# A gated GLU on one core: unit 1's weights from ACT's queue to the end of SP's transposing loads, and t2 ahead of s1 and s2

## Chip, cores and metric

The kernel runs on one core of a Trainium2 chip. The metric is the device time in microseconds of one execution; three executions of the kernel before took 551.66, 552.02 and 553.04 us, the median being 552.02.

A core has five engines that run their own instruction streams and wait for each other by semaphores: PE (TensorE: matmuls out of SBUF into PSUM banks), DVE (VectorE), ACT (ScalarE), POOL (GpSimd) and SP (SyncE, which here only issues DMAs). DMAs are issued from the queue of SP or of ACT, in the order of that queue, and the transfers run on 16 DMA engines.

## The reference

```python
B, S, Dm, Df = 1, 2048, 1024, 3584

def reference(x, w_gate, w_up, w_down):
    g = jnp.einsum("bsd,df->bsf", x, w_gate)
    u = jnp.einsum("bsd,df->bsf", x, w_up)
    h = _gelu(g) * u                      # gelu, tanh form
    return jnp.einsum("bsf,fd->bsd", h, w_down)
```

All arrays are bf16.

## The kernel before

The 2048 rows of x are worked in two passes (`ip`) of 1024 rows, each pass in two halves of 512 rows (`c` = 0 and 1; the "second rows" of the change are half 1 of pass 0). x is kept transposed: `xT[c]` has Dm on the partitions, in 8 blocks of 128 (`ko`). Df is worked in 14 units of 256 columns. For each unit a tile `w` holds 256 columns of w_gate and of w_up (two DMAs of 512 KB, `load_w`); the pool of these tiles has three buffers.

A unit's product is made by Strassen's scheme in Winograd's form: seven block products in place of eight, out of sums of blocks. Sums of x's blocks are `t1` to `t4` (four instructions each) and a cast `tb`; sums of the weights' blocks are `s1` to `s4` (two each, one for gate and one for up) and a cast `sa`. Sums are `TENSOR_TENSOR` instructions with both inputs in SBUF: DVE makes them through the helper of line 90, POOL through that of line 93. The casts are ACT's (line 102). t2 needs t1, s2 needs s1, t4 needs t2, s4 needs s2. After the products DVE adds PSUM banks to snapshots (`sum<-bank,p`, `bank<-bank,p`), ACT applies the gelu, and DVE multiplies gate by up into `hT`.

Unit 0 of pass 0 is different: it is made by plain products (`plain`), first for half 0 and then for half 1, so that PE has work while the sums of x and of unit 1's weights are made. The start goes like this:

- SP's queue: four loads of x's first 512 rows (line 436), which PE transposes (line 443); six loads of unit 0's weights (line 453); eight transposing DMAs for half 1 of x, one for each `ko` (line 447); then, in the units that follow, the weights two units ahead and two loads of w_down's rows per unit (`raw`, line 256).
- ACT's queue: the two loads of unit 1's weights (line 503, issued by `load_w` at line 121), placed after ACT's copy of a transposed block. Then gelu of unit 0's first half, the casts `tb` and `sa`, gelu of the second half, two snapshots, and the two loads of unit 2's weights (line 543, called from `aside(-1)` at the head of unit 1).
- PE: `plain` for half 0 (16 matmuls of 256 columns, 24 of 512), `plain` for half 1 (32 of 512 columns, four banks for each pair of `ko`), then unit 1: its first product (8, out of `w` and half 0 of x), another 8, then s2 by t2, s1 by t1, s3 by t3, s4 by tb, the first product of unit 2, and sa by t4 (8 each).
- DVE: t1, hT of half 0, s1, s2, t2, t3, s3, hT of half 1, two adds, s4, t4, and then the unit's sums and products.

The sums `s` of unit 2 and all later units are made by POOL (`make_s(ahead, pool)`, line 530), which in pass 0 also makes sums `m` of w_down's blocks (`keep`, lines 268 to 270), one `j` per unit and three in the last one (the last two into tiles named `w`). SP stores these to a scratch tensor `td` in HBM (lines 277 and 279). The down projection of the pass (`down`) starts with plain products of hT and raw rows of w_down that SP loads (`fetch12`, line 328) from an agenda by step; three such loads stand in SP's queue ahead of the last stores of `td`, the others behind them.

The order on SP, DVE, POOL and PE is the order in which the program is written, and so is ACT's within the start (`manual_schedule`). Small tiles (`t`, `s`, `g`, `raw` and so on) share one pool of 52 slots.

Of the kernel before, what the change touches and what calls it, by code (L numbers as in the profile page):

```python
# [10 lines left out]
def kernel(  # L11
# [23 lines left out]
    nc = tc.nc  # L35
# [40 lines left out]
    def new_x():  # L76
        return [xpool.tile([P, NKB, N], bf16, name=f"xT{c}") for c in range(2)]
# [17 lines left out]
    def new(eng, a, b, op, name, shape=None, dtype=None):  # L95
        t = slot(shape or [P, N], dtype or f32r, name)
        eng(t, a, b, op)
        return t

    def cast(src, name, shape=None):  # L100
        t = slot(shape or [P, N], f32r, name)
        nc.scalar.copy(out=t, in_=src)  # L102
        return t
# [10 lines left out]

    def load_w(u, queue=nc.sync, pinned=False):
        f0 = u * 2 * P
        w = wpool.tile([P, 2, NKB, 2 * P], bf16, name="w")
        for i, src in enumerate((w_gate, w_up)):  # L120
            got = queue.dma_start(
                out=w[:, i],
                in_=src[:, f0 : f0 + 2 * P].rearrange("(ko ki) f -> ki ko f", ki=P),
            )
            if queue is not nc.sync and not pinned:
                tc.keep_in_program_order(got)
        return w

# [7 lines left out]
    def sums_t(xT):  # L136
        K = range(KH)
        lo, hi = [[xT[c][:, k] for k in K] for c in range(2)], [
            [xT[c][:, KH + k] for k in K] for c in range(2)
        ]  # L140
        return Sums(
            how={
                "t1": lambda q: [new(dve, lo[1][k], lo[0][k], SUB, "t1") for k in K],
                "t2": lambda q: [new(dve, hi[1][k], q["t1"][k], SUB, "t2") for k in K],
                "t3": lambda q: [new(dve, hi[1][k], lo[1][k], SUB, "t3") for k in K],
                "t4": lambda q: [new(dve, hi[0][k], q["t2"][k], SUB, "t4") for k in K],
                "tb": lambda q: [cast(hi[1][k], "tb") for k in K],
            }
        )

    def sums_s(w, eng):
        GU = range(2)
        sh = [P, KH, P]
        a11, a21 = [[w[:, i, :KH, h : h + P] for i in GU] for h in (0, P)]
        a12, a22 = [[w[:, i, KH:, h : h + P] for i in GU] for h in (0, P)]
        return Sums(
            how={
                "s1": lambda q: [new(eng, a21[i], a22[i], ADD, "s1", sh) for i in GU],
                "s2": lambda q: [new(eng, q["s1"][i], a11[i], SUB, "s2", sh) for i in GU],
                "s3": lambda q: [new(eng, a11[i], a21[i], SUB, "s3", sh) for i in GU],  # L160
                "s4": lambda q: [new(eng, a12[i], q["s2"][i], SUB, "s4", sh) for i in GU],
                "sa": lambda q: [cast(a22[i], "sa", sh) for i in GU],
            }
        )
# [11 lines left out]
    def gelu(src):  # L176
        g = slot([P, N], f32, "g")
        nc.scalar.activation(g, src, ACT.Gelu_apprx_tanh)  # L178
        return g

    def times(fb, c, g, u):
        dve(hT[:, fb // NJ, fb % NJ, c, :], g, u, MUL)
# [257 lines left out]
    def turn(xT, xn, c, i, copy):  # L440
        tp = bank[4 + i].bitcast(bf16).rearrange("p (k r) -> p k r", k=NKB)
        for ko in range(NKB):
            nc.tensor.transpose(tp[:, ko, :], xn[i][:, ko * P : (ko + 1) * P], ident)
        copy(out=xT[c][:, :, i * P : (i + 1) * P], in_=tp)
# [17 lines left out]
    xT = new_x()  # L462
# [7 lines left out]
    def plain(ps, c, kos, parts=1):  # L470
        n = N // parts
        for k in range(kos.start, kos.stop, 2):
            for part in range(parts):
                cols = slice(part * n, (part + 1) * n)
                for p, (j, i) in zip(ps, [(j, i) for j in range(2) for i in range(2)]):
                    for ko in (k, k + 1):
                        matmul(
                            p[:, cols],
                            wf[:, i, ko, j * P : (j + 1) * P],
                            xT[c][:, ko, cols],  # L480
                            ko == 0 and part == 0,
                            ko == NKB - 1,
                        )

    def finish(ps, c):
        for j in range(2):
            times(j, c, gelu(ps[2 * j]), ps[2 * j + 1])

    on_dve, on_act = nc.vector.tensor_copy, nc.scalar.copy
    t = sums_t(xT)  # L490
    with tc.manual_schedule(engines={ENG.Activation}):
        def keep_warm(n, cols):
            for _ in range(n):
                nc.tensor.matmul(
                    bank[3][:, :cols], lhsT=warm[:, :P], rhs=warm[:, :cols], start=True, stop=True
                )

        keep_warm(NWARM, N)
        for i in range(NS):
            turn(xT, xn0, 0, i, on_act if i == 1 else on_dve)  # L500
            if i < NS - 1:
                keep_warm(3, 2 * P)
        w = load_w(1, nc.scalar, pinned=True)
        s = sums_s(w, dve)
        plain(bank[0:4], 0, range(0, 2), parts=2)
        plain(bank[0:4], 0, range(2, NKB))
        t.make("t1")
        finish(bank[0:4], 0)
        s.make("s1", "s2")
        t.make("t2", "t3", "tb")  # L510
        s.make("s3", "sa")
        plain(bank[4:8], 1, range(NKB))
        finish(bank[4:8], 1)
# [8 lines left out]
    for ip in range(NPASS):  # L522
        for u in range(1 if ip == 0 else 0, NU):
            js = making(u) if ip == 0 else []

            def prepare():
                nonlocal ahead
                nxt["w"], nxt["s"] = ahead, None
                if u + 1 < NU:
                    nxt["s"] = make_s(ahead, pool)  # L530
                if u + 2 < NU:
                    ahead = load_w(u + 2)
                if ip == 0:
                    fetch_wd(making(u + 1))
                    for j in making(u - 1):
                        store_made(j)
                for j, home in zip(js, ("m",) if len(js) == 1 else ("slots", "w", "w")):
                    keep(j, home)

            def aside(part):  # L540
                nonlocal ahead
                if ahead is None:
                    ahead = load_w(2, nc.scalar)
                if part == 0 and "s4" not in s:
                    s.make("s4")
                    t.make("t4")
# [8 lines left out]
            if u + 1 < NU:  # L555
                w, s = nxt["w"], nxt["s"]
# [26 lines left out]
        if not last:  # L583
            w, t, s = got["w"], got["t"], got["s"]
# [29 lines left out]
```

## Time and profile before

| what | us |
|---|---|
| profiled execution | 553.04 |
| its span, first to last instruction | 551.2 |
| PE busy, share of the span | 536.2 (97%) |
| DVE busy | 322.0 (58%) |
| ACT busy | 243.7 (44%) |
| POOL busy | 279.6 (51%) |
| granted PE clock, mean | 0.994 |
| pass 0, unit 1 and later: start of one unit's s2 products to the next | 12.6 |

The profile's page cuts the span into 40 slices and gives the busy share of each engine in tenths. Two of its rows:

```profile
PE   9899999999999959999999999999999999999997
POOL 0069999999999900000068667777777700000000
```

A slice is 13.8 us. POOL is at work from 32 to 193 us (the units of pass 0) and from 280 to 460 us (those of pass 1); between them lies the first down projection. In a row of the timeline the columns are: start and length in us, engine, line, operation, written tile <- read tiles, shape, count; in brackets the idle time before it and what ended it. In a row of busy time by stretch they are: the stretch, its length, then the busy us of PE, PEld (weight loads), DVE, ACT and POOL with the count of instructions, the granted clock, the mean busy share of the DMA engines, and GB/s.

### The profile page before, as it was taken

Reading aid. Unit: us, or ns where it says so; the run is one execution under the profiler, and the core shown is the slowest. Engines: PE = TensorE matmul, PEld = TensorE weight load, DVE = VectorE, ACT = ScalarE, POOL = GpSimd, SP = SyncE. Lnnn points to the kernel's source line nnn. Section 1 sums busy time; section 2 is a strip of 40 time slices with the busy share of each in tenths; the row PEclk is TensorE's granted clock in tenths of the full one; section 3 lists DMA queues with packets and bytes.
Section 4 is the critical chain, followed back from the end, with each engine's and each line's share of the span. In section 5 each row is a group of like instructions: output and inputs, shape, how many; then the busy total and the mean of one; then the engine's idle time right before and its main releaser. Section 6 shows DMA issues by size and latency. Waiting matters only on the chain.

```text
span 551.2 us, 7303 instructions
## 1 busy us (share of the span) xinstructions
PE 536.2 (97%) x2380; PEld 379.2 (69%) x2414; DVE 322.0 (58%) x490; ACT 243.7 (44%) x427; POOL 279.6 (51%) x248
## 2 busy tenths in 40 slices
PE   9899999999999959999999999999999999999997
PEld 5477777667667624888877777677667775478886
DVE  3794455554555792586874455554555548766830
ACT  3455555455555201155435555455555551114541
POOL 0069999999999900000068667777777700000000
PEclk9999999999999979999999999999999999999999
DMA  9794676667625699999825332222222059463751
GB/s 196 172 243 116 186 200 186 204 190 196 178 96 171 230 339 350 254 231 280 301 88 141 104 90 77 77 77 77 77 78 76 1 158 384 163 224 94 217 195 55
DMA packets 108421, 93.28 MB, mean 169 GB/s; under 512 B 17248, under 2 KB 93024, under 8 KB 108384
## 3 DMA queue, kind: packets, MB, share of 16 engines
q1 hardware_dynamic: 104224, 90.72, 57.0%
q10 hardware_dynamic: 4160, 2.10, 2.0%
q8 instruction: 19, 0.31, 0.2%
q14 instruction: 18, 0.15, 0.1%
HBM read 74.45 MB, written 15.20 MB: 163 GB/s over the span
## 4 chain that ended last, share of the span: by engine, by line
PE 84%; POOL 5%; DMA 5%; issue 2%; SPq 2%; DVE 0%; ACT 0%; POOLq 0%; DVEq 0%
PE bank L111 84%; DMA raw<-in_w_down_dram 3%; POOL s L93 2%; POOL m L93 2%; DMA xT<-in_x_dram 2%; POOL w L93 1%; SPq L447 1%; DMA td<-m 1%; SPq L453 1%; SPq L436 0%; DVE bank L90 0%; DVE hT L90 0%; DVE sum L90 0%; ACT st L407 0%; SPq L279 0%
## 5 line engine op out<-in xcount | busy, mean ns | idle before, releaser
L93 POOL TENSOR_TENSOR s<-w 128x512 fp32r<-128x512 bf16 x100 | 118.1, 1203 | 158.2 <-DVE t L90 87.2
L111 PE MATMUL bank<-t,s 128*128 128x512 f32 x648 | 157.1, 398 | 0.0
L111 PEld LDWEIGHTS bank<-t,s 128*128 128x128 f32 x648 | 121.7, 188 | 27.7
L107 ACT COPY p<-bank 128x512 f32<-128x512 f32 x124 | 71.4, 588 | 108.7 <-PE bank L111 108.7
L111 PE MATMUL bank<-xT,w 128*128 128x512 bf16 (+1 forms) x476 | 111.0, 376 | 3.8 <-DMA xT<-in_x_dram 1.9
L90 DVE TENSOR_TENSOR hT<-g,bank 128x512 bf16<-128x512 f32 x112 | 76.7, 687 | 55.0 <-ACT g L178 46.9
L90 DVE TENSOR_TENSOR sum<-bank,p 128x512 f32<-128x512 f32 x54 | 37.3, 691 | 88.5 <-PE bank L111 87.1
L111 PEld LDWEIGHTS <-w 128*128 128x128 bf16 x504 | 45.0, 98 | 61.4 <-issue 15.6
L178 ACT ACTIVATE g<-sum 128x512 f32<-128x512 f32 x81 | 51.3, 633 | 55.4 <-DVE sum L90 53.6
L111 PE MATMUL bank<-q 128*128 128x512 f32 x240 | 58.9, 389 | 0.0
L111 PE MATMUL bank<-t,sa 128*128 128x512 f32 x216 | 58.6, 413 | 0.0
L93 POOL TENSOR_TENSOR s<-w,s 128x512 fp32r<-128x512 bf16 x50 | 57.7, 1178 | 0.0
L111 PE MATMUL bank<-raw,hT 128*128 128x512 bf16 x218 | 50.9, 391 | 6.8 <-DMA raw<-in_w_down_dram 6.5
L93 POOL TENSOR_TENSOR s<-s,w 128x512 fp32r<-128x512 f32 x50 | 57.3, 1170 | 0.0
L111 PE MATMUL bank<-tb,s 128*128 128x512 f32 x216 | 53.3, 389 | 0.0
L111 PEld LDWEIGHTS bank<-q 128*128 128x128 f32 x240 | 45.1, 188 | 9.4
L111 PEld LDWEIGHTS bank<-t,sa 128*128 128x128 f32 x216 | 40.7, 188 | 10.6
L107 ACT COPY u<-bank 128x512 f32<-128x512 f32 x62 | 35.8, 589 | 24.2 <-PE bank L111 24.2
L111 PEld LDWEIGHTS <-hT 128*128 128x128 bf16 x224 | 22.3, 100 | 35.0 <-issue 10.6
L111 PEld LDWEIGHTS bank<-tb,s 128*128 128x128 f32 x216 | 40.5, 188 | 8.4
L102 ACT CAST tb<-raw 128x512 fp32r<-128x512 bf16 x28 | 17.1, 627 | 62.9 <-DMA raw<-in_w_down_dram 26.6
L90 DVE TENSOR_TENSOR bank<-bank,p 128x512 f32<-128x512 f32 x54 | 37.7, 699 | 8.4 <-PE bank L111 7.0
(43 smaller groups left out, 461.2 us busy)
## 6 DMA issues: line engine op xcount, KB each, us to landing
raw<-in_w_down_dram SPq DMA_DIRECT2D x80, 256.0 KB, 3.7
q<-td SPq DMA_DIRECT2D x60, 256.0 KB, 5.1
w<-in_w_gate_dram SPq DMA_DIRECT2D x25, 512.0 KB, 4.2
w<-in_w_up_dram SPq DMA_DIRECT2D x25, 512.0 KB, 5.8
td<-m SPq DMA_DIRECT2D x11, 768.0 KB, 4.5
w<-td SPq DMA_DIRECT2D x6, 1024.0 KB, 8.5
out_dram<-st SPq DMA_DIRECT2D x32, 128.0 KB, 1.7
td<-w SPq DMA_DIRECT2D x2, 768.0 KB, 4.2
```

The lines of the kernel that those rows point to most:

```text
L90: nc.vector.tensor_tensor(out=out, in0=a, in1=b, op=op)
L93: nc.gpsimd.tensor_tensor(out=out, in0=a, in1=b, op=op)
L102: nc.scalar.copy(out=t, in_=src)
L107: nc.scalar.copy(out=t, in_=ps)
L111: nc.tensor.matmul(ps, lhsT=lhs, rhs=rhs, start=start, stop=stop, skip_group_check=True)
L178: nc.scalar.activation(g, src, ACT.Gelu_apprx_tanh)
L447: nc.sync.dma_start_transpose(out=xT[c][:, ko, :], in_=x2[r0 : r0 + N, ko * P : (ko + 1) * P])
L453: got = queue.dma_start(out=wf[:, i, k0:k1], in_=src[k0 * P : k1 * P, 0 : 2 * P].rearrange("(ko ki) f -> ki ko f", ki=P),)
```

## The change

Unit 1's two weight loads no longer go out from ACT's queue after the transposes of half 0. They are issued by SP, right behind the eight transposing loads. In DVE's order t2 moves ahead of s1 and s2 (ACT's cast tb stays ahead of sa); t3 and s3 keep their places after them. The parameter `pinned` goes, since no other call used it. Nothing else in the order of DVE, POOL, PE or SP changes.

```diff
-    def load_w(u, queue=nc.sync, pinned=False):
+    def load_w(u, queue=nc.sync):
...
-            if queue is not nc.sync and not pinned:
+            if queue is not nc.sync:
                 tc.keep_in_program_order(got)
...
-    t = sums_t(xT)
+    w = load_w(1)
+    s, t = sums_s(w, dve), sums_t(xT)
     with tc.manual_schedule(engines={ENG.Activation}):
...
-        w = load_w(1, nc.scalar, pinned=True)
-        s = sums_s(w, dve)
         plain(bank[0:4], 0, range(0, 2), parts=2)
         plain(bank[0:4], 0, range(2, NKB))
         t.make("t1")
         finish(bank[0:4], 0)
+        t.make("t2", "tb")
         s.make("s1", "s2")
-        t.make("t2", "t3", "tb")
+        t.make("t3")
         s.make("s3", "sa")
         plain(bank[4:8], 1, range(NKB))
         finish(bank[4:8], 1)
```

## The prediction

> **What bounds the kernel now.** I read the page first. PE is busy 97% of the span, and its one deep dip stands in the fifteenth slice, where the granted clock falls too. So the question is which chain leads into that dip. The waits of PE, its timeline there, and the chain of waits:
>
> ```profile
> PE bank L111 <- DMA raw<-in_w_down_dram: 6.5, 3, 5.5
> PE bank L111 <- DMA xT<-in_x_dram: 1.9, 2, 1.1
> ...
> 187.54 5.34 PE L111 MATMUL bank<-raw,hT 128*128 128x512 bf16 x23 [0.50 <-DMA raw<-in_w_down_dram]
> 198.40 1.86 PE L111 MATMUL bank<-raw,hT 128*128 128x512 bf16 x4 [5.51 <-DMA raw<-in_w_down_dram]
> ...
> 191.65 1.50 POOL w L93
> 193.15 0.02 issue
> 193.17 0.32 SPq L279
> 193.49 0.05 issue
> 193.53 0.02 SPq L328
> 193.55 0.03 issue
> 193.58 4.77 DMA raw<-in_w_down_dram
> ```
>
> PE stands still from 192.9 to 198.4 because a down-weight load (L328) is queued on SP behind a store (L279) that waits for POOL's last down-weight sum, at 193.15. Going back from there, the waits of POOL between 36 and 194 us list nothing at all, and its busy time is 39.69 of 40 us, then 39.53, 39.45 and 38.14 of 39: POOL works through from its first sum, at 32.36, to 193.15. The end of pass 0 is therefore the start of POOL plus 160.8 us of sums, and PE has 5.5 us to spare before it. Earlier PE work alone gains nothing at 198.4.
>
> What starts POOL? Its first two blocked sums, and the VectorE run beside the first:
>
> ```profile
> 32.36 2.19 POOL L93 TENSOR_TENSOR s<-w 128x512 fp32r<-128x512 bf16 x1 [31.05 <-DMA w<-in_w_gate_dram]
> 280.37 5.08 POOL L93 TENSOR_TENSOR s<-w 128x512 fp32r<-128x512 bf16 x2 [87.22 <-DVE t L90]
> ...
> 31.04 2.49 DVE L90 TENSOR_TENSOR t<-xT,t 128x512 fp32r<-128x512 bf16 x4
> 33.45 0.68 DVE L90 TENSOR_TENSOR hT<-g,bank 128x512 bf16<-128x512 f32 x1
> ```
>
> POOL's sums take 1.16 us in the mean (46 of them). The first took 2.19, so it did its work from about 33.4 on, just when VectorE's run of sums from two SBUF tiles (s4, then t4) gave way to hT, which reads a PSUM bank. The pair at 280.37 took 5.08 where 2.3 is usual, and it too ends 1.1 us per sum after such a run (t, up to 283.3). So POOL's start is 33.4, the end of VectorE's t4, and not the landing of unit 2's weights at 32.3. I infer the block from these two places.
>
> **The change, part by part.** (1) *Unit 1's weights leave ACT's queue, at 10.24, and go on SP behind the eight transposing loads.* In the old order they ran into those loads:
>
> ```profile
> 12.00:13.00 1.00, 1.00 (x6) 0.47 (x5) 0.66 (x1) 0.95 (x2) 0.00 (x0) 1.00 2.10 55
> 13.00:14.00 1.00, 1.00 (x7) 0.41 (x6) 0.00 (x0) 0.73 (x2) 0.00 (x0) 1.00 0.06 6
> ...
> 11.08 6.69 SPq L447 DMA_TRANSPOSE xT<-in_x_dram  x4
> ```
>
> Nearly nothing moves from 12 to 14 us (55 and 6 GB/s). The fourth to eighth transposes land at 17.2, 19.6, 19.8, 20.2 and 20.7, 5.0 to 8.5 us after issue, where the first three took 3.5 to 4.5. A like hole stands at 221 us (70 GB/s), again with transposes under way but without ACT's loads; both holes, and only some of the quiet stretches, have an instruction load on queue q8. So I keep the hole and take away only what follows it, the sharing with ACT's 1 MB. The transposes then land at about 14.5, 15.2, 15.8, 18 and 19.2, in time for PE: the 32 matmuls of x's second rows start at 14.0 and need the last of them at 14.0 + 24 x 0.216 = 19.2. They end at 20.9 instead of 23.1: 2.2 us of PE waits gone.
>
> The price is the landing of the same weights, 16.9 (gate) and 19.2 (up) before. On SP a transpose issues every 1.29 us, so the eighth would be out at 16.2. Two of the eight took 2.0 us in the old run. The one at 12.4 lay in the hole and I let it happen again (+0.75); the one at 15.8 lay beside ACT's load and I don't. Gate is issued at 17.05, up at 17.5. A pair of such loads on an idle SP queue (23.30 and 23.73) took 4.0 and 5.4 us, so gate lands at 21.1 and up at 22.9. Bounds: 22.1 (no slow issue), and 26.4 (both slow, up issued at 18.3 and taking the 8.1 us that it took from ACT). I take 22.9, the nearer row, because nothing else is on the queues then. The next weight load on SP waits until PE has finished with unit 0's weights (20.9), so nothing is held up behind the two that were added; ACT loses two issues of 0.48 and 0.40 us, which nothing waited for.
>
> (2) *VectorE makes t2 before s1 and s2.* Same 490 instructions. Before, s1, s2, t2, t3, s3, hT, the sums, s4 and t4 run without a gap from 17.8. Now t1, hT and t2 follow the landings up to 19.2 + 0.7 = 19.9 and VectorE then waits for the weights. From the second s1 (the up half) to the last t4 are 19 instructions, 0.603 us apart (the t4 row: (2.49 - 0.68)/3). The last t4 starts 18 x 0.603 = 10.85 after that s1. Before, it started at 32.85, so the point at which nothing changes is an s1 at 22.0. With up landing at 22.9 the run is 0.95 us later, and so is t4: POOL may start at 34.35 instead of 33.4.
>
> (3) *PE in unit 1.* Gate's first products at 21.1, up's at 23.0, the next eight until 25.6; the first s2 product starts there (before: 26.5). Then bank 5 is wanted at 28.3 but VectorE's hT frees it at about 29.1, a wait that takes the place of one removed, and PE is left some 0.2 us ahead of before. This is inside the 5.5 us that PE later stands anyway.
>
> (4) *Unit 2's weights* go out behind ACT's second p copy. That is now set by the cast of unit 1's up half: 22.9 + 2.3 = 25.2, against 25.04. But the load ahead of them on SP starts 2.1 us earlier (20.9 for 23.1), so gate may land at 32.3 - 2.1 = 30.2 (bounds: 32.3, nothing gained, and 29.2, the 4.0 us of an unshared load). VectorE's run of s4 and t4 begins 13 x 0.603 after the s1, at 30.8. If gate lands after 30.8, POOL waits out the run: +0.95. If it lands at 30.2, POOL's first sum gets in, holds s4 until 31.4, and the second sum, whose weights land near 32, waits for the end of the run at 35.0 where it stood at 34.5 before: +0.5.
>
> Sum: between +0.5 and +0.95 on POOL's start, so +0.7 on its end and on PE's restart at 198.4. All later work keeps its length. The profiled execution took 553.04 with a span of 551.2; I expect a span near 551.9, and 552.02 + 0.7 = 552.7 on the median (the profiled run is the slowest of the three shown).
>
> A rule against this reckoning: the Trainium skill, page "SBUF — State Buffer", section "SBUF: two separate sides", says that VectorE (with two SBUF inputs) and GpSimd hold their shared ports for one whole instruction, whoever starts first. By it POOL would wait for one VectorE instruction, not for a run; starting near 30.9 it would end 2.5 us earlier, and the sum would be 549.5. The trace has both: from 187 to 194, where POOL is already running, the two alternate; at 32.4 and at 280.4, where POOL comes late, it waits out the run. I go by the two rows at which POOL starts.
>
> **The clock.** The granted clock is 0.50 from 196.02 to 202.84 and 1.00 around it, after the window in which PE was busy 3.69 of 6.83 us. PE works 4.4 us of that at half speed and loses 2.2. With the stall at 5.5 + 0.9 us, the loss stays between some 1.5 and 3.4 us (a whole window at half speed), so it moves the result by -0.7 to +1.2 and I take 0.
>
> **Rivals.** *A late landing decides (slower).* If unit 1's up weights land after 23.65, POOL's start is more than 1.66 us later. For it: SP's issues of 2.0 us, and 7 to 8 us landings of such loads whenever the queues are shared. Against: with ACT's load gone nothing shares. One more slow issue and a landing of 6.3 us (the middle of the window's loads) give up at 24.6: +2.6, 554.6.
>
> *POOL gets in and stays in (faster).* If both halves of unit 2's weights land before VectorE's run, the two alternate as at 187 to 194, some 1.65 us a pair. POOL ends up to 0.8 us earlier. VectorE's t4 is 4 to 6 us late and PE with it, but PE has 5.5 us to spare; the stall at 193 shrinks to 1 or 2 us and the half clock with its 2.2 us may go: -0.8 - 2.2 = 549.0. Against: the up half lands 1.8 us behind gate, so both must be some 1 us earlier than I have them.
>
> *The removed waits reach the end (faster).* If PE and not POOL set the end, 2.2 us come off: 549.8. For it: PE is busy 97%. Against: 5.5 us of idle PE at 198.4, led to by POOL without a single wait.
>
> *The transposes aren't helped*, since the hole at 12 to 14 remains: PE then ends plain work at 22 to 23, still covered by the 5.5 us; the time is the forecast's.
>
> **How the numbers follow.** 0.3% of 552 is 1.66 us, about what a measurement of this kernel can tell from no change. Forecast, with the last rival in it: 0.50, 552.7, own range 551.5 to 553.7. Late landing: 0.30, 554.6. POOL gets in: 0.12. Removed waits reach the end: 0.08. So faster 0.20, same 0.50, slower 0.30. The range leaves out half of the two faster cases and the later part of the late one: 549.6 to 555.2.
>
> **What would show it.** Right: PE's wait for xT at 15 to 20 us gone; up weights landing at 22 to 23.6; VectorE idle just before s1; t4 ending near 34.4; POOL's first or second sum stretched until then; POOL's last sum ending 0.5 to 1 us after 193.15; the stall before 198 a little longer. Wrong: POOL's last sum ending before 192.5 or after 195, or the restart of PE moving while POOL's end does not.

## The result, and the profile after

| | before | after |
|---|---|---|
| median of 4 runs each | 551.95 us (551.66 to 553.04) | 556.37 us (555.12 to 556.68) |
| ratio of the times, 95% interval | | 1.0072 (1.0051 to 1.0093) |
| profiled execution, its span | 553.04, 551.2 | 555.12, 553.3 |

The changed kernel is slower by 4.4 us, where the prediction had +0.7 and a range up to 555.2. The same kernel in six more executions of a later session (e10_after_again) gave 556.08 (554.47 to 558.09) against 552.46: ratio 1.0067 (1.0048 to 1.0085). The profiled execution of the kernel before is the slowest of its four, that of the kernel after the fastest, so the two traces show 2.05 us of the 4.4.

What PE waits for in the kernel after (us in total, times, longest):

```profile
PE bank L111 <- DVE sum L90: 3.9, 1, 3.9
PE bank L111 <- DMA raw<-in_w_down_dram: 3.4, 4, 1.5
...
PE bank L111 <- DMA w<-in_w_up_dram: 0.6, 1, 0.6
PE bank L111 <- DVE hT L90: 0.6, 1, 0.6
PE bank L111 <- DMA w<-in_w_gate_dram: 0.5, 1, 0.5
```

The waits for xT (1.9 us before) are gone, as the change provides; waits for unit 1's weights and for hT, 1.76 us together, stand in their place. The 5.5 us in front of the raw rows have shrunk to 1.05. New is a wait of 3.9 us for a sum of DVE. The timelines of DVE and of POOL where it lies:

```profile
31.00 1.32 DVE L90 TENSOR_TENSOR s<-w,s 128x512 fp32r<-128x512 bf16 x2
32.25 6.33 DVE L90 TENSOR_TENSOR t<-xT,t 128x512 fp32r<-128x512 bf16 x4
38.51 0.67 DVE L90 TENSOR_TENSOR hT<-g,bank 128x512 bf16<-128x512 f32 x1
39.10 0.68 DVE L90 TENSOR_TENSOR sum<-bank,p 128x512 f32<-128x512 f32 x1
```

```profile
30.01 1.17 POOL L93 TENSOR_TENSOR s<-w 128x512 fp32r<-128x512 bf16 x1 [28.71 <-DMA w<-in_w_gate_dram]
31.68 1.68 POOL L93 TENSOR_TENSOR s<-w 128x512 fp32r<-128x512 bf16 x1 [0.50 <-DMA w<-in_w_up_dram]
33.32 3.16 POOL L93 TENSOR_TENSOR s<-s,w 128x512 fp32r<-128x512 f32 x2
36.45 3.16 POOL L93 TENSOR_TENSOR s<-w 128x512 fp32r<-128x512 bf16 x2
39.56 2.30 POOL L93 TENSOR_TENSOR s<-w,s 128x512 fp32r<-128x512 bf16 x2
```

Before, t4 took 2.49 us in DVE's order (31.04 to the 33.45 of hT) and POOL's first sum 2.19. Now t4 takes 6.33 and five of POOL's sums take 1.6 each: the two engines take turns, one sum each in about 1.6 us. POOL is early (its ninth sum starts at 41.82, before at 42.37), DVE is late, and behind t4 stand hT and the `sum<-bank,p` which must have read its bank before PE may put the product of sa and t4 there. PE in the same stretch before:

```profile
26.38 5.84 PE L111 MATMUL bank<-t,s 128*128 128x512 f32 x24
...
35.42 2.19 PE L111 MATMUL bank<-t,sa 128*128 128x512 f32 x8
37.45 1.90 PE L111 MATMUL bank<-xT,w 128*128 128x512 bf16 x8
39.00 5.82 PE L111 MATMUL bank<-t,s 128*128 128x512 f32 x24
```

PE in the kernel after, and its busy time and granted clock in three windows:

```profile
34.26 1.67 PE L111 MATMUL bank<-xT,w 128*128 128x512 bf16 x7
39.84 3.78 PE L111 MATMUL bank<-t,sa 128*128 128x512 f32 x8 [3.90 <-DVE sum L90]
43.42 3.08 PE L111 MATMUL bank<-xT,w 128*128 128x512 bf16 x8
46.15 4.22 PE L111 MATMUL bank<-t,s 128*128 128x512 f32 x17
```

```profile
35.57:38.98 3.41, 0.36 (x2) 0.00 (x0) 3.41 (x3) 0.00 (x0) 3.41 (x3) 1.00 0.64 165
38.98:42.39 3.41, 2.55 (x6) 2.07 (x7) 3.30 (x6) 2.17 (x5) 3.41 (x4) 0.50 0.00 0
42.39:45.80 3.41, 3.41 (x9) 1.34 (x9) 1.79 (x3) 0.54 (x2) 3.41 (x4) 0.50 0.34 103
```

Behind a window in which PE was busy for 0.36 of 3.41 us the granted clock is 0.50 for 6.82 us, the two last rows. Unit 2's s2 products start at 46.15 where they started at 39.00. From unit 1's s2 products (25.62, before 26.38) that is 20.53 instead of 12.62 us, and 7.91 lie between them. The waits are 4.50 of it (3.90, and 0.60 for hT). The 16 products at half clock took 6.31 us (39.84 to 46.15) where they had taken 3.58 (35.42 to 39.00): 2.73 more. The last 0.68 lie at the same two waits: from start to start of the matmuls around them, these places grew by 0.89 and 4.26 us. Every unit after that takes 12.6 us in both kernels, so PE, 7.15 us late at unit 2's s2 products, reaches the down projection at 194.03, 6.49 us late (before, it waited 0.50 us there).

At the end of the pass, the timelines of POOL and SP after, and SP's before:

```profile
187.91 7.29 POOL L93 TENSOR_TENSOR w<-w 128x512 fp32r<-128x512 bf16 x6
```

```profile
191.60 3.95 SPq L279 DMA_DIRECT2D td<-w  x2
195.64 1.38 SPq L328 DMA_DIRECT2D raw<-in_w_down_dram  x2
```

```profile
188.48 5.01 SPq L279 DMA_DIRECT2D td<-w  x2
193.58 1.37 SPq L328 DMA_DIRECT2D raw<-in_w_down_dram  x2
```

POOL's last sum ends at 195.20 (193.14 before), SP issues the store of it and, 0.09 us behind the store in both kernels, the raw load; this lands, and PE restarts at 200.43 (198.40): +2.03. (The profile's own chain names a PE matmul that ends at 195.64 as what released this load; the 0.09 is the same in the kernel before, where nothing of PE ends there.) The first product of the sums q, at 222.06 instead of 220.00, and the span carry the same difference, +2.06 and +2.05. POOL's end is later although POOL began earlier, and the waits of SP's queue and of POOL say why:

```profile
SPq L121 <- PE bank L111: 118.8, 13, 11.5
SPq L256 <- DVE sum L90: 46.7, 9, 6.6
SPq L256 <- POOL m L93: 40.0, 9, 6.5
```

```profile
POOL m L93 <- DMA td<-m: 3.5, 3, 2.0
```

In the kernel before it was:

```profile
SPq L256 <- POOL m L93: 73.4, 9, 9.7
...
SPq L256 <- DVE hT L90: 13.0, 3, 6.8
```

There SP's loads of w_down's rows (line 256) waited for POOL above all, and never for `sum`: POOL set its own pace. In the kernel after, with PE and DVE some 7 us late in every unit, nine of these loads wait for DVE's `sum`, and the loads and the stores of td behind them reach POOL late three times (1.08 us at 77, 0.46 at 116, 1.99 at 181). The sum: -0.55 (ninth sum) + 3.53 - about 1.0 (the last sums took 1.5 to 1.6 us each beside DVE before, 1.17 now) = +2.0 on POOL's end.

### The profile page after: what moved, and what is told of

It is laid out like the page before. It is cut to its first block, busy times and chain, and to the rows that moved or that the text cites. A ratio compares the mean times of both kernels' runs of the same rounds, so it can differ in the third digit from the quotient of the medians.

```text
span 553.3 us, 7308 instructions
## 1 busy us (share of the span) xinstructions
PE 537.5 (97%) x2380; PEld 379.7 (69%) x2414; DVE 323.4 (58%) x490; ACT 243.8 (44%) x427; POOL 280.0 (51%) x248
## 3 DMA queue, kind: packets, MB, share of 16 engines
q10 hardware_dynamic: 2080, 1.05, 0.7%
## 4 chain that ended last, share of the span: by engine, by line
PE 89%; DMA 4%; SPq 3%; DVE 2%; issue 1%; ACT 0%; DVEq 0%
PE bank L111 89%; DMA raw<-in_w_down_dram 3%; SPq L447 2%; DVE t L90 1%; DMA w<-in_w_up_dram 1%; DVE s L90 1%; SPq L453 1%; SPq L436 0%; DVE hT L90 0%; DVE sum L90 0%; ACT st L407 0%; SPq L121 0%; DVEq L90 0%; SPq L328 0%
## 5 line engine op out<-in xcount | busy, mean ns | idle before, releaser
L111 PE MATMUL bank<-t,sa 128*128 128x512 f32 x216 | 60.2, 422 | 3.9 <-DVE sum L90 3.9
L111 PE MATMUL bank<-raw,hT 128*128 128x512 bf16 x218 | 49.0, 379 | 3.7 <-DMA raw<-in_w_down_dram 3.4
```

The source lines that it names most:

```text
L111: nc.tensor.matmul(ps, lhsT=lhs, rhs=rhs, start=start, stop=stop, skip_group_check=True)
```

## The experiments

Ratios are against the kernel before in the same session; its median was 552.25 for e1 to e4, 551.85 for e5 to e8, and 552.46 for e9 to e12.

**e1_gate: keep POOL out until t4 is done.** The kernel after, with one small sum of POOL (128 x 8) that reads t4's last tile, ahead of unit 2's sums; its result is not used.

```diff
+                if ip == 0 and u == 1:
+                    pool(late, t["t4"][3][:, :8], t["t4"][3][:, :8], SUB)
                 if u + 1 < NU:
                     nxt["s"] = make_s(ahead, pool)
```

> The changed kernel, with one small POOL subtraction on t4's last tile ahead of unit 2's sums, so that POOL starts only when VectorE has made t4. Theory (POOL's sums get between VectorE's t4 sums, t4 takes 6.3 us for 2.5, PE waits 3.9 us for the sum behind it and loses its clock): t4 takes 2.5 us again, the 3.9 us wait at 39.8 us goes, POOL starts near 34.5 and ends pass 0 about 1 us later than in the kernel before, 552.5 to 553.5 us. Rival (the late landing of unit 1's weights itself costs the time): the landing stays at 23.2 us, so the time stays at 556 to 557 us.

Measured: 554.89 us (554.63 to 555.39), ratio 1.0043 (1.0028 to 1.0058). The timelines of DVE and POOL, and of PE at the end of the pass:

```profile
31.87 2.49 DVE L90 TENSOR_TENSOR t<-xT,t 128x512 fp32r<-128x512 bf16 x4
34.28 0.68 DVE L90 TENSOR_TENSOR hT<-g,bank 128x512 bf16<-128x512 f32 x1
```

```profile
34.44 0.20 POOL L93 TENSOR_TENSOR late<-t 128x8 fp32r<-128x8 f32 x1 [33.14 <-DVE t L90]
34.60 2.27 POOL L93 TENSOR_TENSOR s<-w 128x512 fp32r<-128x512 bf16 x2
```

```profile
188.28 5.34 PE L111 MATMUL bank<-raw,hT 128*128 128x512 bf16 x23 [1.11 <-DMA raw<-in_w_down_dram]
199.86 4.48 PE L111 MATMUL bank<-raw,hT 128*128 128x512 bf16 x13 [6.24 <-DMA raw<-in_w_down_dram]
```

t4 takes 2.49 us again, PE has no wait of 3.9 us, and the down projection begins at 188.28. So POOL's sums between DVE's are what made t4 late. The time is 2.6 us above the kernel before, where the changed kernel was 4.4 and (e10_after_again) 3.6 above it. What stays is at the end of the pass, which is POOL's again (its last sum ends at 194.59, +1.45; PE restarts at 199.86, +1.46), since POOL now starts 1.20 us later than the 33.40 of before. Of that, 0.84 is t4's end (34.36 for 33.52); the rest lies where the extra instruction stands. I expected 552.5 to 553.5; the direction was right, the size not.

**e2_early: the suspected cause in the kernel before, without the change.** Unit 2's weights go out earlier, ahead of the second gelu; nothing else.

```diff
         s.make("s3", "sa")
+        w2 = load_w(2, nc.scalar, pinned=True)
         plain(bank[4:8], 1, range(NKB))
...
-    ahead = None
+    ahead = w2
```

> The kernel before, with unit 2's weights issued on ACT ahead of unit 0's second gelu and unit 1's snapshots (near 22.9 us for 25.0). Nothing of the change is in it. Theory: both halves land before VectorE's s4 and t4 at 29.8 us, POOL is at work when they come, the six sums take about 1.6 us each, PE waits 4 to 5 us at 36 us and its clock falls: 554 to 558 us. Rival (late weights of unit 1): these land as before, so nothing gets worse: 551 to 552 us, or better since POOL starts earlier.

Measured: 555.07 us (553.44 to 556.78), ratio 1.0049 (1.0030 to 1.0068). DVE's timeline, and PE's:

```profile
31.39 6.34 DVE L90 TENSOR_TENSOR t<-xT,t 128x512 fp32r<-128x512 bf16 x4
```

```profile
38.98 3.68 PE L111 MATMUL bank<-t,sa 128*128 128x512 f32 x8 [4.35 <-DVE sum L90]
42.46 1.94 PE L111 MATMUL bank<-xT,w 128*128 128x512 bf16 x8
44.05 2.20 PE L111 MATMUL bank<-t,s 128*128 128x512 f32 x8
```

SP's loads of line 256 wait 47.2 us for DVE's `sum` here, as in the kernel after; in e1_gate they wait for POOL again (73.4 us, and none for `sum`). The same t4, a wait of the same kind (4.35 us for 3.90) and a loss (2.8 us, where the changed kernel lost 4.4 and 3.6) appear with none of the change's edits in the kernel. What makes the changed kernel slow is that unit 2's weights come earlier against DVE's run of s4 and t4: gate lands at 29.94 for 32.28, up at 31.61 for 34.11, and the run itself begins 1.16 us later (31.00 for 29.84), so that POOL is at work ahead of it.

**e9_early_warm: the wait and the half clock apart.** e2_early, and 18 matmuls into a free bank where PE stood, so that PE is not idle; they compute nothing that is used.

```diff
                     nxt["p1"] = first_product(even if u % 2 else odd, xT, nxt["w"])
+                if ip == 0 and u == 1:
+                    for _ in range(18):
+                        matmul(bank[2], warm[:, :P], warm, True, True)
```

> The kernel before with unit 2's weights early (as e2_early), and 18 matmuls of 512 columns more for PE, into a bank that is free, behind unit 2's first product, where PE stood for 4.35 us in e2_early. They compute nothing that is used. Theory that the price of the wait is the wait and a half clock of its own behind it: VectorE's t4 still alternates with POOL (4 x 1.64 us), PE has no wait of 4 us but is busy for 18 x 0.216 = 3.9 us, there is no granted clock of 0.50 near 39 us, unit 2's s2 products start near 42.5 instead of 44.05, the down projection near 190.4 instead of 191.95, and the time is 0.5 to 2 us below e2_early's 555.07: 553 to 554.5. Rival, the clock falls for another reason: 0.50 near 39 us stays, unit 2's s2 products stay at 44 or later, and the time is 555 or more.

Measured: 554.25 us (552.88 to 556.35), ratio 1.0029 (1.0017 to 1.0042), 0.8 below e2_early; the intervals of the two ratios overlap, so the times alone don't tell them apart. PE's timeline:

```profile
35.47 4.05 PE L111 MATMUL bank<-warm 128*128 128x512 bf16 x18
40.11 2.11 PE L111 MATMUL bank<-t,sa 128*128 128x512 f32 x8 [0.60 <-DVE sum L90]
42.06 1.90 PE L111 MATMUL bank<-xT,w 128*128 128x512 bf16 x8
43.61 2.64 PE L111 MATMUL bank<-t,s 128*128 128x512 f32 x10
```

The clock stays at 1.00 here (it falls only at the end of the pass, at 199.86), and the eight products of sa begin 1.95 us before the next group, where they took 3.48 (38.98 to 42.46) in e2_early. From t4's end to unit 2's s2 products it is 4.74 us (38.87 to 43.61) against 6.32 (37.73 to 44.05): the half clock cost 1.6 us there, for a stretch of 3.41. The products start at 43.61 and not near the 42.5 that I expected, and the down projection at 191.50 and not at 190.4, because POOL and DVE began to take turns 1.1 us later in this execution.

**e3_order and e4_oldorder: one half of the change each.** The first is the kernel before with t2 and tb ahead of s1 and s2; the second is the kernel after with the old order.

```diff
+        t.make("t2", "tb")
         s.make("s1", "s2")
-        t.make("t2", "t3", "tb")
+        t.make("t3")
```

> The kernel before, with only VectorE's order changed (t2 ahead of s1 and s2). Theory: t2 follows the transposes' landings to 20.7 us, the run of s4 and t4 ends about 0.6 us later, still ahead of POOL: 552.0 to 553.2 us. Rival (the order costs the time): 555 us or more.

> The changed kernel with VectorE's old order (s1, s2 ahead of t2); unit 1's weights stay on SP. Theory: s1 waits for weights that land at 21.5 and 23.2 us, t2 is 2.4 us later than in the changed kernel and so are t3, s3, s4 and t4; POOL comes in at 30 us among more of VectorE's two-tile sums, so PE's wait near 36 us grows: 557 to 561 us. Rival (the order is what costs): back to 552 us.

Measured: e3_order 553.10 (552.59 to 554.47), ratio 1.0015 (1.0005 to 1.0025); e4_oldorder 559.39 (553.33 to 560.50), ratio 1.0107 (1.0072 to 1.0142). In e3_order gate lands at 31.15, in the middle of DVE's run: POOL's first sum takes 2.90 us, t4 2.49, and PE, at the down projection 1.4 us earlier (186.15), stands 6.89 us there until the same 198.38. In e4_oldorder t2 stands behind unit 1's late weights as well; POOL is at work ahead of s4, s4 and t4 take turns with it (1.5 to 1.66 us each), PE waits for 1.84 and 4.08 us, and reaches the down projection at 197.6; this execution is the slowest of six, which lie far apart. The loss belongs to the move of the weights, and the new order of DVE takes part of it back.

**e7_warm: a miss.** The kernel after with the 18 matmuls of e9_early_warm.

> The changed kernel with 18 matmuls of a zero tile into a free bank between unit 2's first product and sa by t4, so that PE is busy through the 3.9 us in which it waits. The wait itself stays. Theory (the stall costs its 3.9 us and then some 3 us of half clock): no half clock near 39 us, PE reaches the down projection some 3 us earlier (near 191 us), and the time falls to POOL's own limit, 553 to 555 us. Rival (the half clock is not what PE loses): PE reaches the down projection at 194 us as now, 556 us.

Measured: 555.37 (553.33 to 556.33), ratio 1.0057 (1.0040 to 1.0074). In its profile there was no wait to fill. Its timelines of POOL and of DVE:

```profile
31.21 5.87 POOL L93 TENSOR_TENSOR s<-w 128x512 fp32r<-128x512 bf16 x2 [29.91 <-DMA w<-in_w_gate_dram]
```

```profile
31.26 1.28 DVE L90 TENSOR_TENSOR s<-w,s 128x512 fp32r<-128x512 bf16 x2
32.46 2.48 DVE L90 TENSOR_TENSOR t<-xT,t 128x512 fp32r<-128x512 bf16 x4
```

Two sums of POOL take 5.87 us, the first of them 4.75, and DVE is not slowed at all: POOL waited out the whole run, and the matmuls only cost PE their time. The run says nothing of the price of the clock, but it shows how near the two cases lie. Five of the profiled executions in which nothing holds POOL back, by the landing of unit 2's gate half and the start of DVE's s4 (e6_fetch_after is below):

| kernel | gate lands | first s4 | t4, us each |
|---|---|---|---|
| after | 29.94 | 31.00 | 1.64 |
| e10_after_again | 31.02 | 31.60 | 1.64 |
| e6_fetch_after | 30.82 | 31.54 | 1.64 |
| e7_warm | 31.14 | 31.26 | 0.68 |
| before | 32.28 | 29.84 | 0.68 |

The others lie further out on the same two sides: in e2_early, e4_oldorder and e9_early_warm gate lands 3.4 us or more ahead of s4 and the engines take turns; in e3_order and in e5, e11 and e12 (below) it lands 1.7 us or more behind the start of s4, and POOL waits.

**e10_after_again.** The kernel after, unchanged.

> The changed kernel itself, word for word, in more executions beside the kernel before. Theory (POOL's second sum gets in between s4 and t4 by about 1 us of landing time): its executions lie between 554 and 557, median 555 to 556.5, ratio 1.005 to 1.009; if the profile of this one has unit 2's up weights landing later than the start of t4, t4 takes 0.68 us each and the time is nearer to e1_gate's 554.9. Rival, the loss is an accident of the first session: the ratio's interval includes 1.000.

Measured as told at the top. Its trace has t4 at 1.64 us each, a wait of 4.14 us, the clock at 0.50 for 3.41 us, unit 2's s2 products at 46.01, POOL's end at 195.85 and a span 2.7 above the profiled one of before. The cause is the same in a second execution; the links differ, the half clock most (one window of 3.41 us for two).

**e5, e6, e8, e11, e12: the end of the pass.** If PE's restart there is held by raw loads that queue behind the stores of td, more loads ahead of the stores should pay, and should show what the change costs without that cover. Six loads instead of three (e5 on the kernel before, e6 on the kernel after, e8 on e1_gate, e11 on e3_order), and eight (e12, on the kernel before, with 16):

```diff
-        at(max(-1, 2 * n - 6), fetch12, n)
+        at(max(-1, 2 * n - 12), fetch12, n)
```

> The kernel before, with the plain down-weight loads (line 328) three steps of two further ahead, so that six of them and not three stand in SP's queue ahead of the stores that wait for POOL. Theory (in the kernel before, POOL's end at 193 us sets the restart at 198.4 us, and 5.5 us of PE's time and some 2 us of clock are lost there): the stall at 193 us goes or falls under 1 us, no half clock stands there; part may come back as waits for DMA, which moves 370 to 380 GB/s right after: 544 to 549 us. Rival (PE sets the end and the stall is not in the way): 551 to 552 us.

> The changed kernel with the same three loads further ahead. Theory: with the end of pass 0 no longer set by POOL, PE's lateness of 6.5 us on reaching the down projection is no longer covered by the stall of the kernel before, so this is 4 to 7 us above the kernel before with the same edit: 549 to 555 us, and further apart from it than 556.4 is from 552. Rival (the end is set by something else after 198 us): the two differ by 4 us, as they do now, or less.

> The changed kernel with both edits: POOL held until t4, and the down-weight loads further ahead. Theory: no wait of PE at 36 us and none at 193 us; PE reaches the down projection 0.7 us later than in the kernel before, so 0 to 2 us above the kernel before with the loads further ahead, and clearly below the kernel before. Rival: as for the others, no gain over the kernel before.

> The kernel before with only the order of the change (t2 ahead of s1 and s2) and with six raw loads in front of the stores of td. Theory that the end of pass 0 is no longer held by POOL once the loads are in front: PE's earlier arrival at the down projection (186.2 for 186.8) may be kept, 547.3 to 548.2. Rival, POOL's later start still decides by the rest of the raw loads: 548.2 to 549.3, as much above e5_fetch_before's 548.20 as e3_order stood above the kernel before (0.85).

> The kernel before with eight raw loads, not six, in front of the stores of td. Theory that the 3.2 us in which PE still waits for raw rows in e5_fetch_before are loads behind stores: two more in front remove 1 to 2 us, 546 to 547.5. Rival, the slots of the pool or SP's queue are taken in earlier units and SP's later loads, or POOL's stores, come late: 548 to 551.

| kernel | median (range), us | ratio (95%) | first q product in the trace |
|---|---|---|---|
| e5_fetch_before | 548.20 (547.25 to 549.92) | 0.9933 (0.9918 to 0.9948) | 214.60 |
| e6_fetch_after | 552.94 (549.05 to 554.34) | 1.0005 (0.9986 to 1.0025) | 219.57 |
| e8_gate_fetch | 550.60 (550.16 to 552.31) | 0.9976 (0.9966 to 0.9986) | 217.47 |
| e11_fetch_order | 549.37 (548.03 to 550.90) | 0.9936 (0.9919 to 0.9953) | 216.24 |
| e12_fetch_more | 547.37 (546.54 to 548.71) | 0.9906 (0.9891 to 0.9921) | 213.17 |

The last column is of one execution each; those of e8 and e12 are the slowest of their runs, and that of e11 the second slowest. PE's timelines in e5_fetch_before and in e12_fetch_more:

```profile
186.76 10.53 PE L111 MATMUL bank<-raw,hT 128*128 128x512 bf16 x48
197.96 3.61 PE L111 MATMUL bank<-raw,hT 128*128 128x512 bf16 x16 [0.67 <-DMA raw<-in_w_down_dram]
```

```profile
186.75 19.47 PE L111 MATMUL bank<-raw,hT 128*128 128x512 bf16 x88
207.67 3.61 PE L111 MATMUL bank<-raw,hT 128*128 128x512 bf16 x16 [1.45 <-DMA raw<-in_w_down_dram]
```

48 matmuls without a pause instead of 23, then 88; in neither is the clock at 0.50 behind them. Both beat the kernel before, and e12_fetch_more has the lowest time of all (its interval and that of e5 touch). Its first q product is 6.8 us earlier than before, its span only 4.7 (546.6): the rest is given back behind it, 0.9 us of that in new waits for q. With six loads ahead the change costs 4.7 us (e6 against e5, within the 4 to 7 expected, but hardly more than the 4.4 without), and 2.4 with POOL held back (e8 against e5, where I expected up to 2): the cover changed little of the change's price. The twelve executions of e6 show that price come and go: three have a mean clock of 1.000, so no half clock, and 549.05 to 550.11 us, and the nine others 0.994 to 0.997 and 551.46 to 554.34. That fits POOL waiting out the run in the three, as in e7_warm; only one of the nine has a trace. What the order alone costs on top of six loads is not settled: e11 is 1.2 us above e5, but in another session, and the ratios (0.9936 and 0.9933) can't be told apart. Its 549.37 lies just above both expected ranges. The trace of e11 speaks for the rival: POOL's second sum starts at 35.70 and its last ends at 194.75, the next raw load lands 1.68 us too late, and the first q product is 1.6 us behind that of e5.

## Why the prediction failed

**What failed is step (4), and the price of the rival that stood against it.** Step (4) let POOL's second sum wait for the end of DVE's run, so that t4 would end at 35.0 and POOL's end move by some 0.7. In its place the second sum started at 31.68, the engines took turns, t4 ended at 38.58, and POOL's end moved by 2.06. The prediction had this case as a rival, "POOL gets in and stays in", with the right mechanism, the right 1.65 us a pair and the right 4 to 6 us of delay for t4, and called it faster: 549.0, chance 0.12. Three things were wrong in its price:

- *"PE has 5.5 us to spare"* was set against 4 to 6 us of delay. The wait itself was 3.9, but it brought a half clock of its own: 2.7 us by the working above, and 1.6 for a shorter stretch by e2_early against e9_early_warm. The prediction's part on the clock looks only at the stall that was there before, not at one behind a new wait. With the wait for hT the delay was 7.9 from unit to unit, and 6.5 at the down projection. Taken alone this would have cost 0.98 at the restart (PE's 23 matmuls end at 199.38, the old restart was at 198.40); the 2.03 are POOL's, by the next point.
- *"The end of pass 0 is the start of POOL plus 160.8 us."* This holds while POOL sets its own pace, and e1_gate shows it: from the first sum's work to the last sum's end it is 160.0 us there (34.60 to 194.59) and 159.7 before (33.40 to 193.14; the 160.8 counts from 32.36, the start of the first sum's record). It does not hold once DVE is late, since SP's loads of w_down's rows wait for DVE's reads too. POOL began 0.55 us ahead and ended 2.06 behind. I had taken an absence of waits for independence.
- *"The half clock with its 2.2 us may go."* It went, and brought nothing: the raw loads behind the restart cost PE 2.34 us (0.43, 1.46, 0.45) where they had cost 0.45. As I read it, PE at full speed only met loads for which PE at half speed had come late enough; no run tries this alone.

**Landing times.** Forecast: transposes by 19.2, up weights of unit 1 at 22.9, unit 2's gate half at 30.2. Measured: 18.17, 23.16, 29.94; up landed at 31.61, against "near 32". ACT issued unit 2's gate half at 24.29 (before 25.04, forecast about 25.2), and it took 5.65 us where it had taken 7.24: both steps made it earlier. The hole at 12 to 14 us stayed, as assumed, if less deep (95 and 54 GB/s for 55 and 6). t4's end without POOL was forecast at 34.35 and is 34.36 in e1_gate and 34.94 in e7_warm, so the exact agreement is luck; the first s2 product of before, given as 26.5, is at 26.38.

**The second sum of POOL.** The text let POOL's first sum in and had the second wait for the end of DVE's run, by the two rows at 32.4 and 280.4, against the rule of the Trainium skill, page "SBUF — State Buffer", section "SBUF: two separate sides", that the engine which starts first holds the shared ports for one instruction. At 31.68 the rule was right and the two rows were not: POOL came in between s4 and t4, and then every other turn was its own. The 549.5 that the prediction gave for the rule was wrong even so, since it left out what POOL's turns do to t4. In e7_warm the rows were right. So the regime turned on some tenths of a microsecond, and the forecast's gate half at 30.2, 0.6 us ahead of s4, was on the side where POOL gets in. A chance of 0.12 for that side did not follow from my own numbers.

**The forecast's own chain, alone, was nearly right in the trace.** With POOL held back the trace has t4's end at +0.84 (forecast +0.95) and POOL's end at +1.45, part of it the extra instruction. The median of e1_gate is nevertheless 2.6 above the kernel before, where the two traces differ by 1.45. The profiled execution of before (553.04) is about 0.8 above the median of before in e1's session (552.25); where an execution at the median is faster cannot be read, since only one has a trace. So of the 4.4 us, 2.05 are followed through the traces (2.7 of 3.6 in e10_after_again), and the rest is open. Half clock does not explain it: the three faster executions of the kernel after all have a mean clock of 0.994. It goes with part of the spread, since the slowest of the four has 0.991, and the two slowest of e10_after_again (557.78 and 558.09) have 0.990.

**The other rivals.** The removed waits did not reach the end: 1.9 us of waits for xT became 1.76 of others. A late landing did not happen in the profiled execution.

## What to carry to other kernels

When an engine loses time that another engine's idle time seems to cover, price what the wait does besides being a wait: here a half clock behind it that cost 2.7 us, and loads that wait for the late engine and so slow the one that was thought free. A transfer made earlier is not free either: ask which engine it releases and whose run that engine will break into. And before tuning the start of a pass, look at what holds its end: three to five more loads in front of a waiting store were worth 3.7 to 5.1 us, while no edit at the start that was tried here gained anything.

## What was unexpected on the chip

- VectorE's sums of two SBUF tiles and GpSimd's sums meet in two ways. If GpSimd arrives within a run, its one sum takes 2.19, 2.90 or 4.75 us, until the run is over, and VectorE is not slowed (before, e3_order, e7_warm; in e7_warm its record even starts 0.05 us ahead of the run). If it is at work before the run, the two take turns, each sum of either taking about 1.6 us (after, e2_early, e4, e6, e9, e10). In this second way VectorE's instruction lasts 1.64 for 0.68 alone, GpSimd's 1.60 for 1.17. What decides between the two is not shown: in after GpSimd had paused for 0.50 us and came back inside the run, and still took turns.
- The granted clock falls to 0.50 for 3.41 or 6.82 us, and the stretch begins at the end of a window with little PE work (0.36 of 3.41 us in after, 0.14 of 3.42 in e2_early). The Trainium skill, page "TensorE: Matmul & The Clock Gate", section "Part 1: The HAM clock gate", gives windows of about 3.4 us, half clock after an idle one and full clock after a busy one. The lengths agree. PE need not be wholly idle: cutting all fourteen traces into windows of 3.41 us that fit the changes of the clock, each one at full clock with at most 1.18 us of PE work was followed by half clock, each with 1.74 or more was not, and of three with 1.55 to 1.58 one was.
- Whether one window is lost or two depends on when the wait ends. In after PE came back 0.86 us into the slow window, was busy for 2.55 of 3.41, and a second slow window followed; in e2_early it came back 0.14 us ahead of it, was busy for all 3.41, and the clock rose after one. In the fourteen traces 3.10 us of work or more in a slow window brought the clock back, and 2.55 or less did not.
